# Cutting one store by partitions into 112, 8 and 8 in a channel-attention kernel on one NeuronCore

## The chip, the cores and the metric

The kernel runs on one core of a Trainium2 chip. Its time is the device time of one execution in microseconds (us). Before the change the median of 3 runs is 717.94 us, the lowest 717.83 and the highest 717.94. The profile is one further execution, taken by the hardware profiler.

## What is computed

The input x has 384 x 384 pixels with 384 channels in bf16, 113.2 MB. The mean of each channel over all pixels is multiplied by one weight and put through a sigmoid; the output is x with each channel multiplied by its value:

```python
g = jnp.einsum("bhwc->bc", x) / (H * W)
s = sigmoid(g * w1d[0])        # k = 1, so there is no padding
return x * s[:, None, None, :]
```

No output can be written before the last input has been read, and x doesn't fit into the core's on-chip memory (SBUF). So there are two passes. The second reads what couldn't be kept a second time.

## The kernel before

The 147,456 pixels are dealt to the 128 partitions, 1152 pixels ("rows" of 768 bytes) to each. The rows are two chunks: 785 rows called STREAMED and 367 called KEPT (line 218). An arena of 275 rows per partition holds all data (`arena`).

*Pass one* loads every row. TensorE sums it over partitions with a matrix of ones into PSUM. 784 streamed rows are dropped after that. The others stay in the arena: some raw, most in groups that VectorE packs from four rows into three. ScalarE checks that the packing loses nothing. When the last row is in, ScalarE turns the sum into the sigmoid `s_bf`.

*Pass two* writes the output. Rows in the arena are unpacked and multiplied by `s_bf` in place (`scale`, line 444; VectorE, with GpSimd taking one row in five of larger blocks, `share`, line 452) and stored by `store` (line 465). The arena rows that a store has emptied are used to load the 784 streamed rows again; these are scaled and stored as well.

The order of all this is made by a planner at build time (lines 596 to 830). It steps a model of the transfers and of VectorE. `send` puts a scaled block on a list, and the main loop later calls `store` for it, then books its rows as free (`stored`, line 644). When enough free rows lie together the loop calls `load` (line 235) for streamed rows, and `split` (line 635) cuts a large load into parts that are scaled one after the other. The planner's model is a sum over rows per transfer. It isn't told how a store is cut, so the order of loads, stores and scales is the same before and after the change.

All loads and stores go out on one queue, that of SP, in the order in which the planner calls them. `Flow.add` (line 34) finds each step's dependencies from the arena rows it reads and writes. A load into rows waits for every store that has read them. A store waits for the engine that scaled its rows. A DMA takes one of 24 completion counters in turn (line 26), and waits for the DMA 24 before it on the queue (lines 49 to 52). SP does the waits itself, so a waiting transfer holds back all that are behind it.

A transfer has the 128 partitions as its outermost dimension, and for each partition one unbroken run of rows, both in SBUF and in the output. So far every transfer of x and of the output has spanned all 128 partitions. One list, `THIN` (line 463), cuts one store along its rows.

The store that the change touches is that of 30 streamed rows. They come in one load of 2880 KB, issued at 381.86 us of the span. VectorE scales 24 rows and GpSimd 6. The store goes out at 409.78 us. The next two stores go out at 412.13 and 425.89 us, and the next load at 446.33 us.

Of the kernel before, what the change touches and what calls it, by code (L numbers as in the profile page):

```python
# [131 lines left out]
def kernel(  # L132
# [11 lines left out]
    nc = tc.nc  # L144
    P = nc.NUM_PARTITIONS
# [46 lines left out]
    arena = pool.tile([P, ROWS, C], bf16, name="arena")  # L192
# [11 lines left out]
    of = out.rearrange("b h w c -> (b h w) c")  # L204

    def view(t, r0, n):
        return t[r0 * P : (r0 + n) * P, :].rearrange("(p r) c -> p r c", r=n)

    def rows(lo, n):
        return [("a", r) for r in range(lo, lo + n)]  # L210

    fl = Flow(nc, tc)
# [5 lines left out]
    STREAMED, KEPT = (0, N_STREAM + 1), (N_STREAM + 1, N_KEPT - 1)  # L218
# [77 lines left out]
    def fold(k):  # L296
# [46 lines left out]
        reads=["ones", "w_bf"], writes=["bank0"],  # L343
# [4 lines left out]
        reads=["bank0"], writes=["w_sc"],  # L348
# [36 lines left out]
    for i, bk in enumerate(banks):  # L385
        lo, hi = i * BANK, min((i + 1) * BANK, PS * C)
# [35 lines left out]
    for a, n in [(U, 8), (A, 20), (A + 20, 7), (A + 27, 12), (V, 8), (Y + 1, 6), (T + 5, 4), (T + 2, 3), (T, 2)]:  # L422
# [9 lines left out]
        reads=["bank0", "w_sc"], writes=["s_bf"],  # L432
# [32 lines left out]
    def store(chunk, a, lo, hi):  # L465
        r0, n = chunk
        cuts = THIN[lo] if chunk == KEPT and lo in THIN else (0, hi - lo)
        for i, j in zip(cuts, cuts[1:]):
            step = fl.add(
                "SP",  # L470
                lambda i=i, j=j: nc.sync.dma_start(  # L471
                    out=view(of, r0, n)[:, lo + i : lo + j, :], in_=arena[:, a + i : a + j, :]
                ),
                reads=rows(a + i, j - i), dma=True,
            )
        return step

    def unfold(g, first):

        _, q = GROUPS[g]  # L480
        steps = []
        whole = q == PAIR
        for k in of_group(g)[: 1 if whole else None]:
            _, lo, p = pieces[k]
            n = q if whole else p
            a, at = first + 3 * lo, first + 3 * q + lo
            last = whole or k == of_group(g)[-1]
            steps += unfold_rows(a, at, p, n, int(last and g == BANKED))
        return steps
# [234 lines left out]
    while True:  # L724
# [12 lines left out]
        if dve_at <= now:  # L737
# [4 lines left out]
            if landed and (ahead < PENDING or not can):  # L742
                chunk, a, lo, n, end = landed.popleft()
# [18 lines left out]
        if alongside and alongside[0][0] <= now:  # L762
            _, chunk, a, lo, n = alongside.popleft()
            store(chunk, a, lo, lo + n)
            moves.append([now + LAT, n * ROW + PER_STORE, stored(a, n)])
        while waiting and waiting[0][0] <= now:
            _, n, then, chunk, a, lo, known = waiting.popleft()
            known.append(store(chunk, a, lo, lo + n))
            last_is_load = False
            sent_off += 1  # L770
            moves.append([now + LAT, n * ROW + PER_STORE, then])
# [10 lines left out]
        if bank_at is None and len(line) <= total - BANKS_AT and got and max(got)[0] > PS * 4 // 3:  # L782
            a = max(got)[1]
# [3 lines left out]
            for i, bk in enumerate(banks):  # L787
                lo, hi = i * BANK, min((i + 1) * BANK, PS * C)
# [6 lines left out]
        if got and todo < N_STREAM:  # L795
            n, a = max(got)
            n = min(n, CAP, N_STREAM - todo)
# [62 lines left out]
```

## Time and profile before

| | |
|---|---|
| median of 3 runs | 717.94 us |
| the profiled execution's own time | 717.85 us |
| its span, first to last instruction | 715.6 us |
| VectorE busy | 467.5 us |
| TensorE busy | 221.1 us |
| GpSimd busy | 98.0 us |
| DMA queue q1, share of 16 engines | 99.0% |
| HBM read and written | 190.32 and 113.25 MB |

The span is shorter than the execution's time by what lies before its first and after its last instruction. The share of q1 is the time that its pieces took, added up over the sixteen DMA engines and divided by sixteen spans. In a table of stretches, the DMA share books a piece with all of its time and bytes in the stretch where it starts. So a short stretch can show a share far over 1, or none while pieces still run. Over long stretches the share is the mean load of the engines.

### The profile page before, as it was taken

How to read it: one execution, taken by the hardware profiler on the slowest of the kernel's cores; microseconds unless marked ns; L12 is line 12 of the kernel's file. 1: busy time of each engine (PE TensorE's matmuls, PEld its weight loads, DVE VectorE, ACT ScalarE, POOL GpSimd, SP SyncE). 2: the span in 40 equal slices, each digit the busy share in tenths (PEclk: the TensorE clock that was granted, in tenths of full speed). 3: DMA queues.
4: the chain of work that ended last, by engine and by line, in shares of the span. 5: the costliest groups of instructions: out<-in, count | busy, mean ns of one | idle time of the engine just before them, and what ended most of it. 6: DMA issues, size and time to landing. Idle time of an engine off the chain costs nothing.

```text
span 715.6 us, 2106 instructions
## 1 busy us (share of the span) xinstructions
PE 221.1 (31%) x1279; PEld 0.3 (0%) x3; DVE 467.5 (65%) x383; ACT 116.5 (16%) x97; POOL 98.0 (14%) x46
## 2 busy tenths in 40 slices
PE   4658877999998890000000000000000000000000
PEld 0000000000000000000000000000000000000000
DVE  4600001898989849999999999999940597007840
ACT  3700001576667630000110000000000000000000
POOL 0000000000000005414233431167100000000000
PEclk9899989999999996555555555555555555555555
DMA  9999999999999989999999999999999999999997
GB/s 382 428 446 419 439 431 425 447 422 433 425 430 427 430 351 379 407 418 435 427 428 437 441 422 437 443 435 430 444 414 459 423 431 442 420 435 439 442 426 326
DMA packets 15997, 303.70 MB, mean 424 GB/s; under 512 B 1778, under 2 KB 2418, under 8 KB 5106
## 3 DMA queue, kind: packets, MB, share of 16 engines
q1 hardware_dynamic: 15984, 303.57, 99.0%
q8 instruction: 5, 0.08, 0.0%
q14 instruction: 6, 0.05, 0.0%
q10 hardware_dynamic: 2, 0.00, 0.0%
HBM read 190.32 MB, written 113.25 MB: 424 GB/s over the span
## 4 chain that ended last, share of the span: by engine, by line
DMA 49%; DVE 29%; PE 16%; ACT 1%; issue 1%; DVEq 0%; SPq 0%; another core or an unknown queue 0%; POOLq 0%
DMA arena<-in_x_dram 37%; DVE arena L444 20%; PE bank L246 16%; DMA out_dram<-arena 11%; DVE arena L280 5%; DVE arena L286 4%; ACT arena L317 1%; DVEq L107 0%; SPq L471 0%; SPq L240 0%; ACT s_bf L431 0%; SPq L113 0%; SPq L855 0%; POOLq L107 0%
## 5 line engine op out<-in xcount | busy, mean ns | idle before, releaser
L246 PE MATMUL bank<-arena,ones 128*128 128x384 bf16 x1151 | 200.6, 337 | 37.5 <-DMA arena<-in_x_dram 37.5
L280 DVE TENSOR_SCALAR arena<-arena 128x1536 uint16<-128x1536 uint16 (+2 forms) x199 | 140.5, 751 | 107.1 <-DMA arena<-in_x_dram 100.0
L444 POOL TENSOR_TENSOR arena<-arena,s_bf 128x768 bf16<-128x768 bf16 (+3 forms) x42 | 97.8, 2333 | 426.5 <-ACT bank L435 268.1
L444 DVE TENSOR_TENSOR arena<-arena,bank 128x3072 bf16<-128x3072 bf16 (+13 forms) x61 | 138.0, 2303 | 4.4 <-DMA arena<-in_x_dram 3.7
L444 DVE TENSOR_TENSOR arena<-arena,s_bf 128x5376 bf16<-128x5376 bf16 (+4 forms) x27 | 76.5, 2902 | 94.9 <-DMA arena<-in_x_dram 84.8
L317 ACT ACTIVATE arena<-arena 128x3072 uint16<-128x3072 uint16 (+1 forms) x38 | 102.5, 2696 | 146.2 <-DVE arena L280 146.2
L286 DVE TENSOR_TENSOR arena<-arena 128x3072 uint16<-128x3072 uint16 (+2 forms) x90 | 117.7, 1307 | 12.2 <-PE bank L246 9.3
L561 PE MATMUL bank<-odd,ones 128*128 128x1 bf16 x1 | 0.2, 187 | 259.5 <-DVE odd L556 259.5
L246 PE MATMUL bank<-s_bf,ones 128*128 128x384 bf16 x125 | 22.1, 326 | 0.0
L382 ACT COPY arena<-bank 128x512 uint32<-128x512 uint32 (+2 forms) x8 | 4.2, 533 | 87.4 <-DMA out_dram<-arena 87.3
L317 ACT ACTIVATION_READ_ACCUMULATOR arena<-arena 128x1 f32 x38 | 7.1, 187 | 0.0
L382 ACT COPY bank<-arena 128x512 uint32<-128x512 uint32 (+2 forms) x8 | 3.8, 527 | 0.0
L260 PE MATMUL bank<-arena,ones 128*128 128x384 bf16 x1 | 0.5, 479 | 6.9 <-DMA arena<-in_x_dram 6.9
L431 ACT ACTIVATE s_bf<-bank,w_sc 128x384 bf16<-128x384 f32 x1 | 0.6, 580 | 9.4 <-PE bank L246 9.4
L828 ACT ACT_TABLE_LOAD x1 | 1.3, 1283 | 0.7 <-PEq L844 0.7
L337 DVE MEMSET ones<- 128x128 bf16 x1 | 0.2, 165 | 1.1 <-PEq L844 1.1
L342 PE MATMUL bank<-w_bf,ones 1*128 1x1 bf16 x1 | 0.2, 182 | 2.1 <-DMA w_bf<-in_w1d_dram 2.1
L347 DVE TENSOR_SCALAR w_sc<-bank 128x1 f32<-128x1 f32 x1 | 0.2, 159 | 0.9 <-PE bank L342 0.9
L565 DVE CAST odd_i<-bank 128x1 int32<-128x1 f32 x1 | 0.2, 157 | 0.3 <-PE bank L561 0.3
L561 PEld LDWEIGHTS bank<-odd,ones 128*128 128x128 bf16 x1 | 0.1, 105 | 517.6 <-DVE odd L556 517.6
L435 ACT COPY bank<-s_bf 128x192 uint32<-128x192 uint32 x1 | 0.3, 323 | 0.0
L382 ACT COPY arena<-rest 128x64 uint32<-128x64 uint32 x1 | 0.2, 244 | 0.0
(10 smaller groups left out, 1.4 us busy)
## 6 DMA issues: line engine op xcount, KB each, us to landing
arena<-in_x_dram SPq DMA_DIRECT2D x3, 6912.0 KB, 36.2
out_dram<-arena SPq DMA_DIRECT2D x3, 6912.0 KB, 28.4
arena<-in_x_dram SPq DMA_DIRECT2D x4, 4608.0 KB, 24.2
arena<-in_x_dram SPq DMA_DIRECT2D x6, 3072.0 KB, 19.8
out_dram<-arena SPq DMA_DIRECT2D x6, 3072.0 KB, 21.5
arena<-in_x_dram SPq DMA_DIRECT2D x2, 6144.0 KB, 30.7
arena<-in_x_dram SPq DMA_DIRECT2D x2, 4992.0 KB, 23.4
arena<-in_x_dram SPq DMA_DIRECT2D x1, 8160.0 KB, 26.5
```

The lines of the kernel that those rows point to most:

```text
L246: return pe.add_instruction(mybir.InstMatmult(name=nc.get_next_instruction_name(), ins=[pe.lower_ap(rhs), pe.lower_ap(ones[:])], outs=[pe. ...
L260: return nc.tensor.matmul(acc, lhsT=ones[:], rhs=arena[:, i, :], start=first, stop=last)
L280: lambda: nc.vector.tensor_scalar(out=dst, in0=src, scalar1=s0, scalar2=s1, op0=op0, op1=op1),
L286: "DVE", lambda: nc.vector.tensor_tensor(out=dst, in0=a, in1=b, op=op), reads=reads, writes=writes
L317: lambda: nc.scalar.activation(out=y, in_=y, func=ACTF.Copy, accum_out=seen[:, 2 * k + i : 2 * k + i + 1]),
L337: fl.add("DVE", lambda: nc.vector.memset(ones[:], 1.0), writes=["ones"])
L382: "ACT", lambda: nc.scalar.copy(dst.bitcast(u32), src.bitcast(u32)), reads=reads, writes=writes
L431: lambda: nc.scalar.activation(out=s_bf[:], in_=acc, func=ACTF.Sigmoid, scale=w_sc[:, 0:1]),
L435: "ACT", lambda: nc.scalar.copy(s_ps.bitcast(u32), s_bf[:].bitcast(u32)), reads=["s_bf"], writes=["bank0"]
L444: lambda: vec.tensor_tensor(out=v, in0=v, in1=s[:, None, :].to_broadcast([P, n, C]), op=Op.mult),
L561: lambda: nc.tensor.matmul(votes, lhsT=ones[:], rhs=odd[:], start=True, stop=True),
L828: nc.scalar.preload_act_table(ACTF.Sigmoid)
```

## The change

`store` gets a second, inner loop over ranges of partitions. For every store but one the range is 0 to 128, as before. For a store of 30 rows of the STREAMED chunk there are three ranges: 0 to 112, 112 to 120 and 120 to 128. Each is a DMA of its own on SP's queue with the same reads of arena rows, the same rows of the output and its own completion counter. The later transfers shift by two in the turn of the 24 counters. `store` returns the last of the three steps; for streamed rows nobody uses it but a list that is dropped.

```diff
     def store(chunk, a, lo, hi):
         r0, n = chunk
         cuts = THIN[lo] if chunk == KEPT and lo in THIN else (0, hi - lo)
+        shares = SHARES if chunk == STREAMED and hi - lo == UNEVEN else (0, P)
         for i, j in zip(cuts, cuts[1:]):
-            step = fl.add(
-                "SP",
-                lambda i=i, j=j: nc.sync.dma_start(
-                    out=view(of, r0, n)[:, lo + i : lo + j, :], in_=arena[:, a + i : a + j, :]
-                ),
-                reads=rows(a + i, j - i), dma=True,
-            )
+            for p, q in zip(shares, shares[1:]):
+                step = fl.add(
+                    "SP",
+                    lambda i=i, j=j, p=p, q=q: nc.sync.dma_start(
+                        out=view(of, r0, n)[p:q, lo + i : lo + j, :], in_=arena[p:q, a + i : a + j, :]
+                    ),
+                    reads=rows(a + i, j - i), dma=True,
+                )
         return step
+
+    UNEVEN, SHARES = 30, (0, P - 16, P - 8, P)
```

## The prediction

> **What bounds the kernel now.** I read the page first: the DMA line of the slices, the queues, the chain of waits.
>
> ```profile
> span 715.6 us, 2106 instructions
> DMA  9999999999999989999999999999999999999997
> q1 hardware_dynamic: 15984, 303.57, 99.0%
> DMA 49%; DVE 29%; PE 16%; ACT 1%; issue 1%; DVEq 0%; SPq 0%; another core or an unknown queue 0%; POOLq 0%
> ```
>
> Queue q1 holds the sixteen DMA engines for 99.0% of the span; only the slice between the two passes shows an 8 and the last one a 7. So the time is that of the transfers, and a transfer that takes longer on a DMA engine is paid in full if that engine is among the last to finish. The chain names VectorE for 29%, but that is where SP waits for a scaled block while the DMA engines still have earlier transfers. The table of stretches for pass two says so. Its columns are the stretch, its length, the engines' busy times with counts, the TensorE clock, the DMA share and GB/s:
>
> ```profile
> 395.00:420.00 25.00, 0.00 (x0) 0.00 (x0) 23.93 (x21) 0.00 (x0) 10.61 (x3) 0.50 1.00 433
> 420.00:445.00 25.00, 0.00 (x0) 0.00 (x0) 24.76 (x15) 0.00 (x0) 6.20 (x2) 0.50 1.00 432
> 445.00:700.00 255.00, 0.19 (x1) 0.10 (x1) 157.47 (x81) 0.00 (x0) 33.78 (x18) 0.50 1.01 435
> ```
>
> From 395 to 700 us the share is 1.00 to 1.01: nothing that SP, VectorE or GpSimd does in that time leaves the DMA engines without work. At 435 GB/s each of the sixteen moves 435/16 = 27.2 GB/s.
>
> Then I looked at how they finish, in short stretches at the end. A transfer's piece for one partition is booked, with its bytes and its whole time, where it starts. The last store is the one of 6816 KB, so a piece is 6816 KB / 128 = 54,528 bytes, and lasts 54.5/27.2 = 2.00 us.
>
> ```profile
> out_dram<-arena SPq DMA_DIRECT2D x1, 6816.0 KB, 25.9
> 709.04:709.60 0.56, 0.00 (x0) 0.00 (x0) 0.00 (x0) 0.00 (x0) 0.00 (x0) 0.50 1.57 682
> 709.60:710.20 0.60, 0.00 (x0) 0.00 (x0) 0.00 (x0) 0.00 (x0) 0.00 (x0) 0.50 1.47 636
> 710.50:710.80 0.30, 0.00 (x0) 0.00 (x0) 0.00 (x0) 0.00 (x0) 0.00 (x0) 0.50 0.42 182
> 710.80:711.10 0.30, 0.00 (x0) 0.00 (x0) 0.00 (x0) 0.00 (x0) 0.00 (x0) 0.50 0.42 182
> 711.60:712.00 0.40, 0.00 (x0) 0.00 (x0) 0.00 (x0) 0.00 (x0) 0.00 (x0) 0.50 0.95 409
> 712.00:715.60 3.60, 0.00 (x0) 0.00 (x0) 0.00 (x0) 0.00 (x0) 0.00 (x0) 0.50 0.00 0
> ```
>
> GB/s times length over 54.5 KB counts the pieces that start: 7, 7, 1, 1 and 3. Three of the second seven are followed, one piece time later, by the three that start after 711.6. So the sixteen engines begin their last pieces in this order: seven before 709.60, four by 710.20, one by 710.80, one by 711.10, three after 711.60. **Three engines set the end**, some 2.5 us behind the first seven: they finish near 713.8, and the span ends 1.8 us later, when the completion has arrived and the last waits are through. Seven engines are early, nine late. The share of 1.01 says that a lag, once there, isn't made up.
>
> **The change part by part.** The store concerned is the only one of 2880 KB:
>
> ```profile
> out_dram<-arena SPq DMA_DIRECT2D x1, 2880.0 KB, 21.8
> 409.78 2.68 SPq L471 DMA_DIRECT2D out_dram<-arena  x2
> 409.78 0.34 SPq L471 DMA_DIRECT2D out_dram<-arena  x1
> 412.13 0.33 SPq L471 DMA_DIRECT2D out_dram<-arena  x1
> 404.75 6.22 DVE L444 TENSOR_TENSOR arena<-arena,bank 128x9216 bf16<-128x9216 bf16 x2 [0.69 <-DMA arena<-in_x_dram]
> 404.80 4.56 POOL L444 TENSOR_TENSOR arena<-arena,s_bf 128x2304 bf16<-128x2304 bf16 x1 [6.85 <-DMA arena<-in_x_dram]
> ```
>
> VectorE scales 24 of its rows, GpSimd six, and SP issues it at 409.78. Its piece is 2880 KB / 128 = 23,040 bytes: 0.85 us.
>
> *Issue on SP.* One issue of 0.34 us becomes three: +0.67 us, so SP is done by 410.8 in place of 410.1. The next store leaves at 412.13, after it has waited for its own rows; the 1.3 us between hide it. Without that cover it would cost nothing either, since the transfers queued ahead last until the store lands, 21.8 us after issue. VectorE and GpSimd get no new wait. Cost 0.
>
> *Waits.* SP reuses 24 completion counters in turn, so each later transfer now waits for the one 22 before it by the old count. The next fence has the longest time from issue to landing, 39.6 us, and 48 stores in 420 us: one in 8.7 us, so 22 transfers, even with a third of them loads, reach back some 130 us. The load that refills these rows has three landings to wait for, and one or two more wait instructions of some hundredths of a us. Behind it on SP stand a load and a store:
>
> ```profile
> L471 SPq DMA_DIRECT2D out_dram<-arena x48: 332/333/1268, 268.5 to 688.3; - x48
> DMA to landing us min/median/max: 1.6/15.5/39.6
> 446.33 7.59 SPq L240 DMA_DIRECT2D arena<-in_x_dram  x2
> ```
>
> It leaves at 446.33, held by a store two places after ours, and a later store is still moving. If it left 3 us late the share would drop there only for engines that are early anyway. Cost 0.
>
> *How the bytes lie on the engines.* This alone can move the end. 128 partitions are eight to an engine; 112 can be seven to each. Eight partitions can be at most one to each of eight engines. Two such transfers go either to different eights (every engine has eight pieces again: 0) or to the same eight (these have nine, the others seven: +0.85 and -0.85 us). No row of before shows which, so the end lies between -0.85 and +0.85 us by this part, and it is -0.85 only if the three late engines are all among those relieved. Late ones drawn at random from two halves would be so in 8·7·6/(16·15·14) = 0.1 of cases; but they come within 0.4 us of each other, the mark of one common cause, and seven early engines against nine late ones are nearly halves. I take relief twice as likely as burden, so -0.85; the ends are kept. The two engines before them, about 0.9 and 1.2 us ahead of the three, don't undo that unless they are burdened.
>
> The Trainium skill, "DMA: Bandwidth & Descriptors", section "Why a DMA increments its semaphore by 16 and not by 1", says that a transfer uses the largest number of engines up to 16 that divides its outermost size, and the lowest-numbered ones: 16 for 112, and the same eight for both small ones. By it the sum is +0.85 or -0.85 and never 0; no run here shows it.
>
> **Sum.** 0 + 0 - 0.85 us against the profiled execution: span 715.6 and 2.25 us around it, 717.85, becomes 717.0. The median of the runs, 717.94, is 0.09 above that one, so the forecast is **717.1**; by the upper end of the same case 718.8. (0.2%, about what a measurement of this kernel can tell from no change, is 1.44 us, so both are "same".)
>
> **The rivals.**
>
> *Neighbouring partitions share a way out, and the small transfers jam (slower).* The 27.2 GB/s may belong to a group of partitions rather than to the engine. In a transfer of 128, sixteen engines can work on sixteen groups; eight adjoining partitions lie in few groups. That a DMA engine can be held below its pace though busy, the trace shows:
>
> ```profile
> 283.00:288.00 5.00, 0.00 (x0) 0.00 (x0) 4.90 (x4) 0.00 (x0) 0.00 (x0) 0.50 1.06 369
> 310.00:320.00 10.00, 0.00 (x0) 0.00 (x0) 9.83 (x8) 0.00 (x0) 0.00 (x0) 0.50 0.99 404
> ```
>
> Full share, yet 369 and 404 GB/s against 435; the cause isn't told. Against it: nothing in this trace shows a transfer of few partitions. Price: with eight groups of one, 0.85 us for each small transfer; with one group of eight, 6.8 us. I take four to a group, midway in doublings, and the group's own engine, already at the next store, as a fifth user: 5 x 0.85 = 4.2 us each, 8.5 for two, less 0.85 for the piece that the eight no longer have: +7.6 us on them. If they are the early ones, they have 2.5 us in hand, and the end moves by +5.1; if not, by +7.6. That gives 723.0 to 725.5, with **723.0** as the likelier. If the group serves its users in turn, the last of four waits 3.4 + 0.85 - 0.85 = 3.4 us, and with the lead of 2.5 the end moves by +0.9. It decides as soon as the eight lose more than their lead. The piece of 112 can add to it where seven partitions straddle two groups.
>
> The Trainium skill, "SBUF — State Buffer", section "Door 1: The DMA port swizzle", has such groups: four neighbours and the four 32 partitions on share one port of some 27 GB/s. By it partitions 112 to 119 lie on two ports, and the estimate is the one above. It is the strongest voice against the change.
>
> *The eight that get more hold the three late engines.* Then +0.85: 718.8. For it speaks mere chance; against it the near halves.
>
> *The shares come out even, or the cut does nothing to the engines.* 717.9.
>
> *A new wait empties the queue.* If the refill of those rows waited for a jammed small transfer until the later store is through, the engines would run dry until it begins to arrive, at least the 1.6 us of the shortest landing in the row above: 719.5. The 1.00 in 420 to 445 speaks against it.
>
> **How the numbers follow.** Engines keep their pace and the end moves by one piece or not at all: 0.54 (relief 0.33, burden 0.16, nothing 0.05), own range 716.9 to 718.9. The jam: 0.40, of which 0.02 within 0.2%. The emptied queue: 0.03. Something that gains over 1.44 us: 0.03. So faster 0.03, same 0.56, slower 0.41. The range goes from 716.8 to 724.2; above it I leave about half of the jam's upper branch, below it the unexplained gain.
>
> **What would show it.** In each case the issues list one store of 2520 KB and two of 180 KB in place of that of 2880. Relief: the last three pieces start near 710.9 in place of 711.7. Burden: they start near 712.6. Jam: in the stretch 420 to 445 the share stays near 1.00 but GB/s falls clearly below 432, and pieces of 23 KB take several times 0.85 us; the last store's starts spread over 5 us or more. Emptied queue: the share itself falls after 420. The forecast is wrong if the GB/s of 420 to 445 falls by over a fifteenth (1.7 us of 25, twice one piece).

## The result, and the profile after

The changed kernel takes 724.96 us (median of 6 runs, 722.23 to 725.49), the kernel before 717.94 us beside it (6 runs, 717.38 to 718.24). The ratio is 1.0093, 95% interval 1.0077 to 1.0109: **7.0 us slower**. The forecast was 717.1 us with "same" as likelier, and the time lies above the range's end of 724.2. The rival that is called the jam in the prediction gave 723.0 to 725.5.

First the profiled execution of the changed kernel (its own time is 725.41 us): the page's first line, its queue line, and the issues by size (KB each, median us to landing):

```profile
span 723.2 us, 2109 instructions
q1 hardware_dynamic: 16000, 303.57, 98.7%
out_dram<-arena SPq DMA_DIRECT2D x1, 2520.0 KB, 25.4
out_dram<-arena SPq DMA_DIRECT2D x2, 180.0 KB
```

The same bytes are moved, still at a share of nearly 1. The queue has 16 packets more than before. The 128 pieces of this store are as many as they were; what is added are 16 records of 4 bytes (1794 packets under 512 B in place of 1778). I take them for the writes that count a transfer complete, one per engine used, so that the two small transfers used eight engines each. The Trainium skill's rule in "DMA: Bandwidth & Descriptors", section "Why a DMA increments its semaphore by 16 and not by 1", gives eight engines for eight partitions, and here the trace agrees: 8 + 8 = 16. Whether they are the same eight can't be read from this trace; a run further down shows it for two such transfers.

Now the stretches of pass two of the changed kernel. The columns are those of the prediction's table, with the DMA share and GB/s last:

```profile
395.00:420.00 25.00, 0.00 (x0) 0.00 (x0) 23.93 (x21) 0.00 (x0) 10.77 (x3) 0.50 1.00 432
420.00:445.00 25.00, 0.00 (x0) 0.00 (x0) 24.76 (x15) 0.00 (x0) 6.20 (x2) 0.50 1.00 369
420.00:430.00 10.00, 0.00 (x0) 0.00 (x0) 9.97 (x5) 0.00 (x0) 3.10 (x1) 0.50 1.10 364
430.00:440.00 10.00, 0.00 (x0) 0.00 (x0) 9.93 (x7) 0.00 (x0) 3.10 (x1) 0.50 0.91 341
445.00:492.00 47.00, 0.00 (x0) 0.00 (x0) 40.49 (x23) 0.00 (x0) 17.45 (x9) 0.50 0.99 411
492.00:700.00 208.00, 0.18 (x1) 0.10 (x1) 117.43 (x59) 0.00 (x0) 16.43 (x10) 0.50 1.00 434
```

Up to 420 us hardly anything differs from before (432 GB/s against 433). From 420 to 445 us, while the three transfers are moved, the share is 1.00 as before, but 369 GB/s stand against 432. The DMA engines are all busy and each moves less. That is the sign that the prediction named for the jam, and a fall by a seventh, where it had called itself wrong from a fifteenth on. The loss there is (432 - 369)/435 x 25 = 3.6 us of sixteen engines' work. It isn't spread evenly over the engines. A second, smaller loss follows up to 492 us: 411 GB/s, where the kernel before ran at 433. From 492 us on it is 434 against 436. The two stretches of before:

```profile
445.00:492.00 47.00, 0.00 (x0) 0.00 (x0) 46.76 (x27) 0.00 (x0) 23.30 (x13) 0.50 1.00 433
492.00:700.00 208.00, 0.19 (x1) 0.10 (x1) 110.72 (x55) 0.00 (x0) 10.49 (x6) 0.50 1.01 436
```

So after 492 us both kernels run at full pace, and what was lost stays lost. SP's issues of the changed kernel show where it is passed on. The load that left at 446.33 us before leaves 6.5 us later, since it waits for a store behind the jam:

```profile
452.79 0.34 SPq L240 DMA_DIRECT2D arena<-in_x_dram  x1
```

The records of the landings, and of the pieces, give the same in other words (us of the span; worked out from the trace):

```
last landing of                       before    changed    difference
the store before (4608 KB)            424.7     425.6       +0.8
the next store (2400 KB)              437.3     443.7       +6.4
the second load after it (6144 KB)    487.3     494.9       +7.6
the last store (6816 KB)              714.2     721.8       +7.6

pieces of 23,040 bytes in this store  before: 128 of 0.855 us
                                      changed: 85 of at most 0.9, 43 longer, up to 6.3 us
```

The records also say which pieces pay. Added up, the cut store's pieces take 50.2 us more than 0.855 each, those of the store before it 0.9 us more than their usual 1.364 each, and those of the next store 7.7 us more than their usual 0.714 each. The sum over sixteen engines is 58.8/16 = 3.7 us, which matches the loss of the stretch. Nearly all of it falls on the cut store's own pieces.

So +6.4 us come at the jam itself, and +1.2 us at the starts of the two loads after it, where pieces are longer than usual again. By then the engines are up to 8 us apart (the 16 landings of the next store spread from 435.5 to 443.7 us), so that some load while others still store; that this lengthens the pieces is likely, as the prediction's stretches with 369 and 404 GB/s had loads and stores under way at once too, but no run tests it. At the end the last pieces of the sixteen engines start over 5 us, where they did over 2.8:

```profile
712.00:714.50 2.50, 0.00 (x0) 0.00 (x0) 0.00 (x0) 0.00 (x0) 0.00 (x0) 0.50 1.11 480
714.50:716.50 2.00, 0.00 (x0) 0.00 (x0) 0.00 (x0) 0.00 (x0) 0.00 (x0) 0.50 0.76 327
716.50:717.50 1.00, 0.00 (x0) 0.00 (x0) 0.00 (x0) 0.00 (x0) 0.00 (x0) 0.50 0.51 218
719.30:720.00 0.70, 0.00 (x0) 0.00 (x0) 0.00 (x0) 0.00 (x0) 0.00 (x0) 0.50 0.18 78
720.00:723.20 3.20, 0.00 (x0) 0.00 (x0) 0.00 (x0) 0.00 (x0) 0.00 (x0) 0.50 0.00 0
```

The last one (78 GB/s x 0.70 us, one piece of 54.5 KB) starts after 719.3 us; before, the last three started at 711.6 to 712.0.

### The profile page after: what moved, and what is told of

Same layout as the page of the kernel before. It is cut to its first block, busy times and chain, and to the rows that moved or that the text cites. A ratio compares the mean times of both kernels' runs of the same rounds, so it can differ in the third digit from the quotient of the medians.

```text
span 723.2 us, 2109 instructions
## 1 busy us (share of the span) xinstructions
PE 222.3 (31%) x1279; PEld 0.3 (0%) x3; DVE 467.8 (65%) x383; ACT 116.5 (16%) x97; POOL 98.2 (14%) x46
## 2 busy tenths in 40 slices
DMA packets 16013, 303.70 MB, mean 420 GB/s; under 512 B 1794, under 2 KB 2434, under 8 KB 5122
## 4 chain that ended last, share of the span: by engine, by line
DMA 56%; DVE 22%; PE 16%; ACT 1%; issue 0%; DVEq 0%; SPq 0%; another core or an unknown queue 0%; POOLq 0%
DMA arena<-in_x_dram 41%; DVE arena L444 17%; PE bank L246 16%; DMA out_dram<-arena 15%; DVE arena L280 3%; DVE arena L286 2%; ACT arena L317 1%; DVEq L107 0%; SPq L473 0%; SPq L240 0%; ACT s_bf L431 0%; SPq L113 0%; SPq L859 0%; POOLq L107 0%
```

## The experiments

The theory at this point: pieces from adjoining partitions that several engines read at once slow each other down (the jam). The rivals: three transfers cost more than one; the uneven dealing of pieces to engines; and, within the jam, which of its parts does it, and whether it lies on the side of SBUF or of the output in HBM. All experiments are edits of the one store (or load) of 30 streamed rows. The diffs show only the lines that tell one from the other, and the comments in them are added here; the inner loop over `SHARES` is as in the change, with slices of partitions in place of bounds. Those that leave rows unwritten say so in their expectation. Each ratio is against the kernel before on the same chip, with its 95% interval.

### Three transfers, cut along the rows

```diff
         cuts = THIN[lo] if chunk == KEPT and lo in THIN else (0, hi - lo)
+        if chunk == STREAMED and hi - lo == 30:
+            cuts = (0, 26, 28, 30)
```

> The 30-row store goes as three transfers again, but cut along its rows (26, 2 and 2 rows), each over all 128 partitions. If the loss comes from partitions that share a way out of SBUF (jam): 0, since every transfer lies as the one of 128 did. If it comes from three transfers in place of one (issues, waits, counters): +7 us as in the changed kernel. If from the pieces being dealt unevenly to the engines: 0.

Measured: 718.04 us, ratio 0.9998 (0.9988 to 1.0007). Three issues on SP, three counters and the waits on them cost nothing that can be seen. The steps "issue on SP" and "waits" of the prediction hold.

### 112 and 16: every engine has eight pieces again

```diff
+    UNEVEN, SHARES = 30, (slice(0, P - 16), slice(P - 16, P))
```

> Two transfers, of 112 and 16 partitions: seven pieces and one piece for each of sixteen engines, so that every engine has eight again. Uneven dealing: 0. Jam: sixteen adjoining partitions lie on four ways out, and 16 x 23,040 bytes over 4 x 27.2 GB/s take 3.4 us in place of 0.85, more where the ways' own engines use them too; with what the 112 lose by themselves +2.5 to +6 us.

Measured: 725.20 us, ratio 1.0099 (1.0082 to 1.0116), as slow as the changed kernel, and with +7.2 us over the +2.5 to +6 given for the jam. The queue has 16,000 packets, 16 more than before, so by the count above the transfer of 16 used sixteen engines, one piece each. The dealing is even, and uneven dealing isn't what costs.

### Four eights, adjoining or four apart, behind a transfer of 96

```diff
+    UNEVEN, SHARES = 30, (slice(32, P), slice(0, 8), slice(8, 16), slice(16, 24), slice(24, 32))  # adjoining
+    UNEVEN, SHARES = 30, (slice(32, P), slice(0, 32, 4), slice(1, 32, 4), slice(2, 32, 4), slice(3, 32, 4))  # four apart
```

> Five transfers: partitions 32 to 127, then 0 to 7, 8 to 15, 16 to 23 and 24 to 31. Eight engines have 6 + 4 = 10 pieces, the others 6. Uneven dealing: the end moves by -1.7 to +1.7 us. Jam: each small transfer has eight partitions on two ways out, five users to a way, 4.2 us each; 17 us for four in place of two pieces (1.7 us) makes the eight late by 10 to 15 us, and the end moves by +8 to +13 us.

> As the kernel with partitions 32 to 127 and four transfers of eight, but each of the eight takes every fourth partition of 0 to 31 (0, 4, ... 28, then 1, 5, ... 29, and so on), so that it lies on eight ways out if four neighbours share one. Engines have 10 and 6 pieces as there. Uneven dealing: the same time as with adjoining eights. Jam: the four small transfers run at full pace, -1.7 to +1.7 us and what the 96 lose by themselves; 6 us or more below the kernel with adjoining eights.

Measured: adjoining 725.78 us, ratio 1.0106 (1.0089 to 1.0123); four apart 723.81 us, 1.0090 (1.0066 to 1.0114). Neither expectation held: the adjoining ones lose 7.7 us, just under the jam's price of 8 to 13, and the spread ones lose nearly as much (5.8). The two kernels share the transfer of 96 partitions, so the suspicion fell on that large part itself. It wasn't run alone; the next runs take the parts of the changed kernel one by one.

### Only the 112, and only the eights

```diff
+    UNEVEN, SHARES = 30, (slice(0, P - 16),)                       # the 112 alone
+    UNEVEN, SHARES = 30, (slice(P - 16, P - 8), slice(P - 8, P))   # adjoining eights alone
+    UNEVEN, SHARES = 30, (slice(0, 32, 4), slice(1, 32, 4))        # eights four apart alone
```

> The store of partitions 0 to 111 alone; the 30 rows of the last 16 partitions are left out and not written. Every engine has seven pieces in place of eight. If the jam is all in the two transfers of eight: -0.85 us against the kernel before. If the 112 jam by themselves, because seven partitions to an engine no longer lie on that engine's own way: +2 to +5 us, most of what the changed kernel loses.

> Only the two small transfers, of partitions 112 to 119 and 120 to 127; the 30 rows of partitions 0 to 111 are left out and not written. The eight engines that move them have two pieces in place of eight, the others none. Dealing alone: -5.1 to -6.8 us. Jam in the eights: 3.4 to 4.2 us each, 6.8 to 8.5 for the eight engines in place of the 6.8 of eight pieces, so 0 to +1.7 us on them; with a lead of up to 2.5 us the end moves by -2.5 to +1.7.

> Two small transfers of eight partitions that are four apart: 0, 4, ... 28 and 1, 5, ... 29; the 30 rows of the other 112 partitions are left out and not written. As many pieces to each engine as with the adjoining eights. Dealing alone: the same time as there. Jam: eight different ways out, full pace, -5.1 to -6.8 us, so 3 to 7 us below the adjoining eights.

Measured: the 112 alone 722.69 us, ratio 1.0080 (1.0049 to 1.0111); adjoining eights 719.79 us, 1.0028 (1.0017 to 1.0039); eights four apart 712.69 us, 0.9930 (0.9914 to 0.9947).

The 112 lose 4.9 us where one piece less should gain 0.85. Their four runs lie far apart, two near 720.8 and two near 725, so the size is uncertain, but all are slower than the whole store; in the traced one (720.64) 24 of the 112 pieces are longer than 0.9 us, up to 3.7. The queue has 16 packets fewer than before, as many as there are pieces left out, so the 112 used all sixteen engines. The eights four apart come out at -5.1 us, which agrees with six pieces of 0.855 fewer on the engines that keep two; the interval, -3.8 to -6.2, wouldn't tell it from seven. That it is the same eight engines twice, the records show: each of the second eight pieces starts 0.857 or 0.858 us after one of the first eight. The adjoining eights, the same bytes in as many pieces, are 7.1 us slower than that and even slower than the whole store. Both parts of the change jam by themselves. Together they lose 7.0 us, less than the two losses added (5.7 and 7.1); how they overlap wasn't taken apart.

The stretch from 420 to 430 us, first with adjoining eights, then with eights four apart:

```profile
420.00:430.00 10.00, 0.00 (x0) 0.00 (x0) 9.97 (x6) 0.00 (x0) 3.79 (x2) 0.50 1.02 289
```

```profile
420.00:430.00 10.00, 0.00 (x0) 0.00 (x0) 9.96 (x6) 0.00 (x0) 3.59 (x2) 0.50 0.98 423
```

At the same share 289 GB/s stand against 423. In the records of the pieces, the sixteen adjoining ones take 1.1 to 5.1 us, on average 4.0; the sixteen spread ones 0.855 us each.

### The side of SBUF or the side of HBM

Two small transfers read one set of partitions and write the output rows of another:

```diff
-                    out=view(of, r0, n)[:, lo + i : lo + j, :], in_=arena[:, a + i : a + j, :]
+                        out=view(of, r0, n)[part, lo + i : lo + j, :], in_=arena[src, a + i : a + j, :]
+    UNEVEN, SHARES = 30, ((slice(112, 120), slice(0, 32, 4)), (slice(120, 128), slice(1, 32, 4)))  # (out, in): from spread
+    UNEVEN, SHARES = 30, ((slice(0, 32, 4), slice(112, 120)), (slice(1, 32, 4), slice(120, 128)))  # (out, in): to spread
```

> Two small transfers that read SBUF partitions four apart (0, 4, ... 28 and 1, 5, ... 29) and write the output's rows of partitions 112 to 119 and 120 to 127, so those get other partitions' values; the 30 rows of partitions 0 to 111 are left out and not written. If the jam is on the side of SBUF: no jam, 712.7 as with both sides spread. If it is on the side of HBM: 719.8, as with both adjoining.

> The other way round: two small transfers that read the adjoining SBUF partitions 112 to 119 and 120 to 127 and write the output's rows of partitions 0, 4, ... 28 and 1, 5, ... 29, which get those values; the rest of the 30 rows is left out and not written. If the jam is on the side of SBUF: 719.8. If on the side of HBM: 712.7.

Measured: from partitions four apart to adjoining output 713.03 us, ratio 0.9926 (0.9909 to 0.9942); from adjoining partitions to spread output 719.97 us, 1.0028 (1.0018 to 1.0037). This decides it for the store: **the jam is on the side of SBUF**. Where the rows lie in HBM makes no difference that can be seen. The stretch of 420 to 430 us, for "from spread" and then "to spread":

```profile
420.00:430.00 10.00, 0.00 (x0) 0.00 (x0) 9.96 (x6) 0.00 (x0) 3.44 (x2) 0.50 0.99 426
```

```profile
420.00:430.00 10.00, 0.00 (x0) 0.00 (x0) 9.97 (x6) 0.00 (x0) 3.17 (x2) 0.50 1.01 297
```

### The load cut in place of the store

The load of these rows goes as 112, 8 and 8 partitions, and what reads the rows waits for all three; the store is whole.

```diff
+            for p, q in ((0, P - 16), (P - 16, P - 8), (P - 8, P)):
                 ... (cut)
+                            out=arena[p:q, a : a + hi - lo, :], in_=view(xf, r0, n)[p:q, lo:hi, :]
```

> The store is whole again; the load of the same 30 streamed rows is cut into 112, 8 and 8 partitions, and the scaling waits for all three. If a way jams for data coming in as it does for data going out: pieces of several us and +5 to +8 us, as with the cut store. If only reading from SBUF jams: within 0.5 us of the kernel before.

Measured: 726.40 us, ratio 1.0114 (1.0097 to 1.0131). The load's 128 pieces take 1.61 us on average, up to 2.87, while those of the whole store stay at 0.855 to 0.860. So a load cut in this way jams as well. That it is the side of SBUF here too is likely, but the two sides weren't parted for a load. The load is moved earlier than the store, and the low stretch moves with it:

```profile
395.00:420.00 25.00, 0.00 (x0) 0.00 (x0) 14.78 (x13) 0.00 (x0) 7.46 (x2) 0.50 1.01 285
420.00:445.00 25.00, 0.00 (x0) 0.00 (x0) 24.76 (x16) 0.00 (x0) 9.29 (x3) 0.50 1.00 431
```

### Halves: adjoining or interleaved

```diff
+    UNEVEN, SHARES = 30, (slice(0, 64), slice(64, P))         # halves
+    UNEVEN, SHARES = 30, (slice(0, P, 2), slice(1, P, 2))     # even and odd partitions
```

> Two transfers of 64 partitions; each gives every engine four pieces, as many as before in all. Uneven dealing: 0. Jam: partitions 0 to 63 lie on half of the ways out and 64 to 127 on the other half, so two engines share each way and each transfer takes 64 x 23,040 / (8 x 27.2 GB/s) = 6.8 us; 13.6 for both in place of 6.8, and the end moves by +4 to +7 us (less than 6.8 where early engines take their share while late ones are still at the store before).

> The whole store as two transfers of 64 partitions, the even and the odd ones. If four neighbours share a way and each engine takes partitions that follow one another in the transfer, every engine has two groups of four to itself: no jam, within 0.5 us of the kernel before. If partitions 32 apart share as well: two engines to a way as with the halves, +4 to +8 us.

Measured: halves 725.28 us, ratio 1.0111 (1.0087 to 1.0134); even and odd partitions 718.24 us, 1.0003 (0.9994 to 1.0013). Here a store is cut by partitions and costs nothing. All 128 pieces of the interleaved cut take 0.855 us; those of the halves take 1.46 us on average. The stretch of 420 to 445 us, halves first:

```profile
420.00:445.00 25.00, 0.00 (x0) 0.00 (x0) 24.76 (x15) 0.00 (x0) 6.20 (x2) 0.50 1.00 337
```

```profile
420.00:445.00 25.00, 0.00 (x0) 0.00 (x0) 24.76 (x15) 0.00 (x0) 6.21 (x2) 0.50 1.00 430
```

So the cut by partitions is not itself the cost, and neither is a transfer of fewer than 128. What matters is which partitions a transfer takes; the likely reason is that it settles which ones the engines are at together, which the records don't name.

### Which partitions share

```diff
+    UNEVEN, SHARES = 30, (slice(64, 96, 4), slice(65, 96, 4))   # four apart, upper half
+    UNEVEN, SHARES = 30, (slice(0, 64, 8), slice(1, 64, 8))     # eight apart
+    UNEVEN, SHARES = 30, (slice(0, 16, 2), slice(1, 16, 2))     # two apart
+    UNEVEN, SHARES = 30, (slice(0, 64, 4),)                     # sixteen, four apart
```

> As the kernel with two small transfers of eight partitions four apart, but of the upper half: 64, 68, ... 92 and 65, 69, ... 93; the 30 rows of the other 112 partitions are left out and not written. If ways out are shared by groups of four and belong to no engine, each of these eight ways is also that of one of the other eight engines, which is at the next store by then: two users, each at half pace, pieces of up to 1.7 us in place of 0.855; four pieces' time for two, and the end comes up to 1.7 us later than with the lower eight (714.4 against 712.7). If it is neighbourhood alone that jams, or if a way serves any engine at full pace: pieces of 0.855 us and 712.7 again.

> Two small transfers of partitions eight apart, 0, 8, ... 56 and 1, 9, ... 57; the 30 rows of the other partitions are left out and not written. If four neighbours and the four that lie 32 on share a way: four ways with two engines each, pieces of 1.7 us, 714.4. If two engines on a way don't slow each other, or if it is neighbours alone that share: pieces of 0.855 us, 712.7.

> Two small transfers of partitions two apart: 0, 2, ... 14 and 1, 3, ... 15; the 30 rows of the other 112 are left out and not written. If four neighbours share one way of 27 GB/s: two engines to each way, pieces of about 1.7 us, 714 to 715. If only eight neighbours or more share: nearer to the adjoining eights, 717 or more. If two engines on a way do no harm: 712.7.

> One transfer of sixteen partitions, 0, 4, ... 60, one piece to each of sixteen engines; the 30 rows of the others are left out and not written. If partitions 32 apart share a way: eight ways with two engines each, a piece of 1.7 us in place of eight of 0.855: -5.1 us against the kernel before. If not: -6.0 us.

Measured, with the pieces of 23,040 bytes from the records of the trace:

```
                           time us   ratio (95%)               pieces: mean, longest us
adjoining (112 to 127)     719.79    1.0028 (1.0017, 1.0039)   3.97, 5.09
two apart (0 to 15)        714.21    0.9949 (0.9932, 0.9966)   1.21, 2.10
four apart (0 to 29)       712.69    0.9930 (0.9914, 0.9947)   0.855, 0.855
four apart (64 to 93)      714.15    0.9949 (0.9932, 0.9965)   0.88, 0.98
eight apart (0 to 57)      714.17    0.9942 (0.9926, 0.9959)   1.11, 1.98
sixteen, four apart        713.62    0.9935 (0.9918, 0.9951)   0.855, 0.855
```

Within four partitions, closer means longer: 0.855 us four apart, up to 2.1 two apart, 4.0 on average and up to 5.1 side by side. By an estimate from the prediction's 27.2 GB/s, five engines on one way would give 4.2 us and two would give 1.7; the sizes fit groups of four neighbours roughly.

Whether the partitions 32 apart share a way with such a group as well, as the recorded expectations assume, isn't settled: the runs point both ways. For it speak the eights eight apart, where 0 and 32, 8 and 40 and so on are in one transfer: seven pieces of sixteen are longer than 0.86 us, up to 1.98. The halves fit it too, as 64 adjoining partitions would then have half of the ways, if each engine takes four that follow one another; how a transfer of 64 is dealt isn't in the trace. Against it speak three runs. Of the sixteen partitions 0, 4, ... 60, ten pieces start within 0.855 us of one another, so that at least two pairs 32 apart overlap, and none is slowed. Of the upper eights, expected at up to 1.7 us, only six pieces are longer than 0.86 us, by 0.13 us over 0.855 at most. And the even and odd partitions, expected at +4 to +8 us by such sharing, lose nothing, though this again hangs on how they are dealt.

The times of these kernels don't settle it. The upper eights, at 714.15 us, come out where sharing would put them (714.4), but by luck: their pieces are hardly longer. They and the sixteen end 1.5 and 0.9 us later than the lower eights for other reasons too, since pieces are long again in them later, with the upper eights around the start of the next load, at 444 to 456 us. That may also be why the sixteen gain only 4.3 us, where 5.1 or 6.0 were expected.

## Why the prediction was wrong

**The profile before was read rightly.** The DMA engines bound pass two, nothing is made up later, and the last engine sets the end: the 7.6 us that are lost by 495 us are still there to the tenth at the last store's landing.

**Issue on SP, waits: 0.** They held; the cut along rows shows it (0.9998). The later leaving of the refill load (452.79 in place of 446.33) is a consequence of the jam, not of the added wait.

**How the bytes lie on the engines: this step failed.** I priced a piece at 0.85 us whichever engine moves it and wherever it comes from, as the stretches of before from 395 us on had it, and then asked only which engine gets more of them. In every row of before, however, all transfers of x and of the output span the 128 partitions, so whichever engine is paired with which partitions, that likely never changes. The trace couldn't show that the pace belongs to the pairing as much as to the engine. By the runs the dealing agrees with what I said (six pieces of 0.855 are 5.1 us, measured with the eights four apart: 5.1, with an interval of 3.8 to 6.2). But which partitions are taken is worth far more: in the changed kernel 43 of 128 pieces are longer, up to 6.3 us, 50 us in all. The relief of late engines, on which the value of 717.1 rested, was never to be seen; whether it would exist without the jam wasn't tested.

**The rival had the right mechanism and nearly the right size.** +5.1 to +7.6 us were given for it; +7.0 were measured. That the size fits is partly luck. The sum put the whole price on the two eights and only mentioned the 112. In the runs the 112 alone already lose 4.9 us, the eights alone 7.1 against spread ones, and the two don't add up. The fifth user that it counted is hardly seen either: with the adjoining eights alone, all sixteen of their pieces are long, 49.9 us in all, but only nine of the 128 of the next store, 5.0 us in all. How a way divides its pace stays open. Where the same price was put on other cuts it was somewhat low: +7.2 us for 112 and 16 (up to +6 given), +7.5 for the halves (up to +7), +8.7 for the load (up to +8).

**The chances: 0.54 to 0.40 should have been the other way round.** One result doesn't measure a chance, but the reasons on record do not bear these out. Against the jam I had only that the trace shows no transfer of few partitions, which is no evidence. For it stood stretches of the trace in which full share went with 369 and 404 GB/s, that is, that an engine's pace isn't its own, and a page of the Trainium skill that named the mechanism. That page, "SBUF — State Buffer" of the Trainium skill, section "Door 1: The DMA port swizzle", was right about neighbours. By it 128 partitions reach all ways and 64 adjoining ones half of them; the halves, which moved 337 GB/s over the stretch against 430 interleaved, fit that. Its further statement that partitions 32 apart share a way isn't borne out by the sixteen four apart, all of whose pieces take 0.855 us, while the eights eight apart, with pieces of up to 1.98 us, would fit it; here that stays open.

## What to carry to other kernels

Cut a DMA along its rows, not by ranges of partitions: three transfers over all 128 partitions cost nothing, while one store cut into 112, 8 and 8 cost 0.9% of a kernel of 718 us. If it must be cut by partitions, cut it into the even and the odd ones: that is the only cut of the whole store by partitions that cost nothing here. Small transfers of partitions four apart kept their pace, but 96 partitions with four of them beside still cost 5.8 us. And before moving pieces between engines to even out a lag, ask whether their pace comes from the engine or from what it reads; a trace in which the pairing never changes can't tell.

## What the runs showed of the hardware

- A piece of 23,040 bytes takes 0.855 us in a transfer over all 128 partitions, over the even or odd ones, or over eight that are four apart (0 to 29); in the store cut into 112, 8 and 8 it takes up to 6.3 us. The DMA share stays at 1.00 all the while, so that of the two figures of a stretch only GB/s gives it away (369 against 432).
- For a store the slowing is on the side of SBUF: 720.0 us from adjoining partitions into spread output rows, 713.0 from spread partitions into adjoining rows. A load cut in the same way is slowed too (726.4 us); its side wasn't tested.
- The slow pieces are those of the cut transfer: with two adjoining eights alone 49.9 us are added to their sixteen pieces and 5.0 to the 128 of the next store.
- A transfer of 112 partitions is slow by itself, +4.9 us (interval +3.5 to +8.0) with seven eighths of the bytes, although it uses all sixteen engines.
- Even and odd partitions in two transfers are as fast as one transfer: 1.0003 (0.9994 to 1.0013).
